# Giving each pair of heads its own order of TensorE work in a fused attention and rational-MLP kernel

## The chip, the cores and the metric

The kernel runs on one core of a Trainium2 chip. The metric is the device time of one execution in microseconds (us); the number compared is the median of several runs.

## The reference

Attention with a soft cap on the scores, over 4 batches of 12 heads, 448 positions and head dimension 64, feeds an MLP whose activation is a rational function.

```python
scores = scale * np.matmul(q, k.transpose(0, 1, 3, 2))
scores = cap * np.tanh(scores / cap)
scores = scores - np.max(scores, axis=-1, keepdims=True)
attn = np.exp(scores)
attn = attn / (np.sum(attn, axis=-1, keepdims=True) + 1e-09)
out = np.matmul(attn, v)                 # 4 x 12 x 448 x 64
x = out.transpose(0, 2, 1, 3).reshape(1792, 768)
h = x @ w_in                             # 768 x 2048
P = a[0] + a[1] * h + a[2] * h * h + a[3] * h * h * h
Q = 1.0 + abs(b[0]) * abs(h) + abs(b[1]) * h * h
y = (P / (Q + 1e-6)) @ w_out             # 2048 x 768
```

## The kernel before, in words

The kernel has two parts. **Attention** takes the 48 heads as 24 pairs, numbered from 0. For one pair, p, TensorE does these pieces, each of which is one entry in the kernel's lists:

- `k` and `q` (`prep_k`, `prep_q`): four transposes each (L343, L345, L366), which bring keys and queries of a pair to come into a score buffer. VectorE takes them out again in two instructions each (L350, L351, L381, L384), as a high and a low part.
- `s0`, `s1`, `s2` (`scores`, L429): the scores of 128 keys each, six matmuls of 448 columns that use half of the array's rows; they run two at a time, so six are three steps. Every odd pair has a fourth tile, `score3`, of twelve matmuls, for the last 64 keys of both pairs. ScalarE takes each tile out with a tanh (L440), and exponentiates it in place in SBUF (L457); VectorE adds a pair's tiles up for the softmax sums (L463).
- `pv` (L511): the product of a pair's exponentials with its values; `tails` (L528): the same for the fourth tile of two pairs. VectorE copies the results out (L535).
- `sums`, `sums4` (`norm`, `norm4`; L556, L594): the softmax sums of two or four pairs, which go through SBUF and a DRAM tensor `dn` and come back, inverted and broadcast, by DMA; VectorE multiplies with them (L627).

There are three score buffers in PSUM, printed as ps_127, ps_128 and ps_129 in the orders below (`slot`: an even pair's s0, s1, s2 go to the first, second and third; an odd pair's s0 to s2 and score3 to the second, third, first and second). The transposes for a later pair of the same parity use the first buffer when that pair is even, the third when it is odd. Two more banks, `pv` and `mi`, hold the products and the sums. Exponentials lie in a ring of six tiles, so two pairs of three. The early weights of the MLP are made ready between the pairs (L789 to L822).

The second part, the **MLP**, works in 32 units: `stage1` multiplies one 128-wide slice of `w_in` with 896 tokens (36 matmuls, 18 of 512 and 18 of 384 columns, each number split in a high and a low part so that three products are summed); `rational` computes the activation on ScalarE and VectorE; `stage2` multiplies with `w_out` (L928), and ScalarE or VectorE takes the result out (L955, L961). The first four units have nothing between their matmuls and are issued slice by slice (L858), the others in two halves (L843).

A planner, `Plan`, sets the order on each engine. Every operation is added with an engine, a cost in ns and the keys that it reads and writes; `flush` then walks a model of the engines in time, with a fixed latency between each two of them, and takes of the ready operations the one that was added first (some with a head start, `early`). All of TensorE's attention pieces write a common key, "turn", so that on TensorE they stand exactly in the order in which they were added; that order comes from `visits`, one fixed list for even pairs and one for odd ones:

```python
            if not p % 2:
                return [s0, s1, s2, *new, (pv, p - 1), (tails, p - 1)]
            sums = (norm, p // 2 - 1)
            ...
            four = [(norm4, p // 2 - 2)] * (p % 4 == 1)
            return [s0, s1, s2, (self.scores, p, 3), *four, (self.softmax, p, 3), *new, (pv, p - 1)]
```

`new` is the `k` and `q` of pair p + 2. In the first two pairs `fill` adds eight matmuls that compute nothing that is used (L405).

Of the kernel before, what the change touches and what calls it, by code (L numbers as in the profile page):

```python
# [23 lines left out]
NE = 6  # L24
# [22 lines left out]
WARM2 = (2, 1, 3)  # L47
FILL = (4, 4)
Q_ACT = ()
# [23 lines left out]
class Plan:  # L73
# [7 lines left out]
    def __init__(self):  # L81
        self.ops = []
        self.wr, self.rd = {}, {}
        self.n = 0
        self.free = [4500.0, 4600.0, 3700.0, 3700.0, 9900.0]
        self.dma_free = 11000.0
        self.where, self.over = {}, {}
# [160 lines left out]
class Body:  # L248
# [11 lines left out]
    def __init__(self, tc, io, cst, bounded):  # L260
# [15 lines left out]
        self.NG = self.NF // self.NCH  # L276
        self.plan = Plan()
        self.loaded = {(0, 0), ("v32", 0), ("v", 0)}
# [53 lines left out]
    def prep_k(self, p):  # L332
# [15 lines left out]
        self.busy(p, 0)  # L348
        self.op(PE, 440 + SHAPE_NS, tk, self.raw_keys(p, "rk"), [bk, "turn"], early=E_TR)
        self.op(DVE, dve_ns(512), lambda: nc.vector.tensor_copy(S[:, 1, :], pk), [bk], [K("kh")], early=E_PR)  # L350
# [3 lines left out]
    def prep_q(self, p):  # L354
# [18 lines left out]
        self.busy(p, 1)  # L373
        self.op(PE, 390, tq, self.raw_keys(p, "rq"), [bq, "turn"], early=E_TR)
        self.busy(p, 2)
# [25 lines left out]
    def fill(self, n):  # L401

        z = self.io["arena_r"][:, 0:512]
        for _ in range(n):
            self.op(PE, 213, lambda: self.nc.tensor.matmul(self.PS[0][:, 1], z[:, 0:128], z, start=True, stop=True),  # L405
                    [], [("ps", 0), ("psb", 0), "turn"])
# [8 lines left out]
    def scores(self, p, n):  # L415
# [8 lines left out]
        def run():  # L424
# [5 lines left out]
            return m  # L430
        first = n == 0 or p % 2 and n == 2
        self.op(PE, SC_NS * len(sets) + TURN_NS * first, run, [k for name, _ in sets for k in K(name)], w, early=E_SC)
# [18 lines left out]
    def exp(self, p, n, src, sk, e, ek):  # L451
# [7 lines left out]
        if n in (0, 3):  # L459
            return  # L460
        es, ks = self.es[p % NES], [("es", p % NES)]
        a, ak = self.etile(p, 0) if n == 1 else (es, None)
# [34 lines left out]
    def pv(self, p):  # L497
# [16 lines left out]

        self.op(PE, PV_NS + SHAPE_NS, run, [("rv", ring_of(g), 0)] + [t[1] for t in tiles], [pk, "turn"])

    def pv_tails(self, p):
# [13 lines left out]

        self.op(PE, TAIL_NS, run, [("v32", ring_of(g), 0), ("v32", ring_of(g), 1), ek], ["pv", "mi", "turn"])
        for x in range(2):
# [4 lines left out]
    def norm(self, k):  # L538
# [19 lines left out]

        self.op(PE, D_NS + SHAPE_NS, sums, [("es", (2 * k + x) % NES) for x in range(2)] + [tk, "ones"], [dk, "turn"])
        self.op(DVE, dve_ns(448), lambda: nc.vector.tensor_copy(DB, D), [dk], ["db"], early=E_EV)  # L560
# [19 lines left out]
    def norm4(self, k):  # L580
# [15 lines left out]

        self.op(PE, D4_NS + SHAPE_NS, sums, [*es, *(t[1] for t in tails), "ones"], [dk, "turn"])
        self.op(DVE, dve_ns(448), lambda: nc.vector.tensor_copy(DB, D), [dk], ["db"], early=E_EV)
# [42 lines left out]
    def attention(self):  # L641
# [33 lines left out]
        def visits(p):  # L675
# [10 lines left out]
            if p == 0:  # L686
                return [s0, s1, (k, 1), (q, 1), s2, (self.fill, FILL[0])]
            if p == 1:
                return [s0, (self.fill, FILL[1]), s1, (k, 2), s2, t, (q, 2), (k, 3), (q, 3), (pv, 0)]
            if not p % 2:  # L690
                return [s0, s1, s2, *new, (pv, p - 1), (tails, p - 1)]
            sums = (norm, p // 2 - 1)
            if p == P1 - 1:
                return [s0, s1, (pv, p - 1), sums, s2, t]
            four = [(norm4, p // 2 - 2)] * (p % 4 == 1)
            return [s0, s1, s2, (self.scores, p, 3), *four, (self.softmax, p, 3), *new, (pv, p - 1)]

# [127 lines left out]
    def stage1(self, u, between=None):  # L825
# [508 lines left out]
```

## Time and profile before

| what | us |
|---|---|
| runs of the kernel before | 659.46, 660.10, 660.89 |
| median | 660.1 |
| the profiled execution: its time | 659.91 |
| the profiled execution: its span, first to last instruction | 657.9 |
| TensorE (PE) busy in the span | 647.8 |
| VectorE (DVE) busy | 541.9 |
| ScalarE (ACT) busy | 442.2 |

The attention part ends on TensorE at 185.86 us of the span, the first four units at 214.47 us, the last matmul after 651 us. An engine's busy time counts a matmul until its modelled end, which overlaps the next one, so the length of a block of matmuls is best read as the time from its first start to the first start of the next block.

### The profile page before, as it was taken

Reading aid. Unit: us, or ns where it says so; the run is one execution under the profiler, and the core shown is the slowest. Engines: PE = TensorE matmul, PEld = TensorE weight load, DVE = VectorE, ACT = ScalarE, POOL = GpSimd, SP = SyncE. Lnnn points to the kernel's source line nnn. Section 1 sums busy time; section 2 is a strip of 40 time slices with the busy share of each in tenths; the row PEclk is TensorE's granted clock in tenths of the full one; section 3 lists DMA queues with packets and bytes.
Section 4 is the critical chain, followed back from the end, with each engine's and each line's share of the span. In section 5 each row is a group of like instructions: output and inputs, shape, how many; then the busy total and the mean of one; then the engine's idle time right before and its main releaser. Section 6 shows DMA issues by size and latency. Waiting matters only on the chain.

```text
span 657.9 us, 9767 instructions
## 1 busy us (share of the span) xinstructions
PE 647.8 (98%) x3820; PEld 542.0 (82%) x3820; DVE 541.9 (82%) x662; ACT 442.2 (67%) x531; POOL 85.0 (13%) x141
## 2 busy tenths in 40 slices
PE   8999999999999999999999999999999999999996
PEld 5555555655478899999999999999999999999996
DVE  4789899899679987977987897899699789969653
ACT  5899999999857867875457466646646565663560
POOL 4013222321200000020012002101200210120030
PEclk9999999999999999999999999999999999999999
DMA  7757864943230332195158118614821671481086
GB/s 170 186 138 171 203 163 100 199 119 85 59 86 22 128 141 92 51 197 113 48 106 158 49 49 152 158 43 86 166 68 49 128 142 60 95 170 33 1 139 203
DMA packets 79095, 74.45 MB, mean 113 GB/s; under 512 B 48456, under 2 KB 67264, under 8 KB 79040
## 3 DMA queue, kind: packets, MB, share of 16 engines
q1 hardware_dynamic: 68240, 48.68, 25.7%
q0 software_dynamic: 9648, 24.80, 22.5%
q8 instruction: 32, 0.52, 0.3%
q10 hardware_dynamic: 1152, 0.25, 0.2%
q14 instruction: 23, 0.19, 0.1%
HBM read 47.98 MB, written 25.65 MB: 112 GB/s over the span
## 4 chain that ended last, share of the span: by engine, by line
PE 82%; DVE 6%; ACT 4%; DMA 3%; issue 3%; POOL 0%; SPq 0%; DVEq 0%; POOLq 0%; ACTq 0%
PE ps L843 31%; PE ps L928 17%; PE mi L928 9%; PE pv L928 9%; PE ps L429 6%; PE mi L511 3%; DMA arena_r<-dn 2%; ACT etiles L440 2%; PE mi L594 1%; PE pv L511 1%; ACT etiles L457 1%; PE pv L528 1%; PE ps L343 1%; DMA dn<-arena_f 1%; PE ps L366 1%
## 5 line engine op out<-in xcount | busy, mean ns | idle before, releaser
L843 PE MATMUL ps<-arena_r,ring 128*128 128x512 f32 (+1 forms) x924 | 207.6, 363 | 0.0
L843 PEld LDWEIGHTS ps<-arena_r,ring 128*128 128x128 f32 x924 | 167.7, 188 | 17.5
L295 POOL DMA_DIRECT2D out_dram<-arena_f x49 | 42.0, 863 | 423.6 <-ACT arena_f L955 423.6
L928 PE MATMUL ps<-arena_r,etiles 128*128 128x384 f32 x462 | 89.7, 335 | 0.6 <-ACT arena_f L955 0.5
L457 ACT ACTIVATE etiles<-etiles,acap 128x896 f32<-128x896 f32 x84 | 85.5, 1053 | 0.2
L440 ACT ACTIVATE etiles<-ps 128x896 f32<-128x896 f32 x84 | 74.7, 921 | 13.9 <-PE ps L429 13.7
L928 PEld LDWEIGHTS ps<-arena_r,etiles 128*128 128x128 f32 x462 | 80.8, 188 | 1.3 <-ACT arena_f L955 0.8
L928 PE MATMUL mi<-arena_r,etiles 128*128 128x384 f32 x231 | 77.2, 336 | 0.0
L928 PE MATMUL pv<-arena_r,etiles 128*128 128x384 f32 x231 | 77.0, 335 | 0.0
L429 PEld LDWEIGHTS ps<-arena_r 64*128 64x128 f32 x576 | 51.0, 184 | 25.2 <-ACT etiles L457 7.8
L889 ACT ACTIVATE arena_f<-ps,b 128x896 f32<-128x896 f32 x32 | 32.3, 1009 | 54.8 <-PE ps L843 54.7
L429 PE MATMUL ps<-arena_r 64*128 64x448 f32 x576 | 67.7, 376 | 1.2 <-DVE arena_r L384 0.9
L789 ACT ACTIVATE arena_f<-arena_f 128x768 f32<-128x768 f32 x32 | 29.4, 918 | 44.1 <-DMA arena_f<-in_moe_w_out_dram 31.0
L901 ACT CAST etiles<-arena_f 128x896 fp32r<-128x896 f32 x32 | 30.3, 946 | 42.0 <-DVE arena_f L900 42.0
L893 DVE SCALAR_TENSOR_TENSOR arena_f<-arena_f,bab 128x896 f32<-128x896 f32 x32 | 36.8, 1150 | 23.8 <-ACT arena_f L890 23.8
L898 DVE SCALAR_TENSOR_TENSOR arena_f<-arena_f,one 128x896 f32<-128x896 f32 x32 | 36.7, 1148 | 11.3 <-ACT arena_f L896 11.3
L928 PEld LDWEIGHTS pv<-arena_r,etiles 128*128 128x128 f32 x231 | 43.3, 188 | 0.6
L928 PEld LDWEIGHTS mi<-arena_r,etiles 128*128 128x128 f32 x231 | 43.3, 188 | 0.6
L928 PE MATMUL ps<-ring,etiles 128*128 128x384 f32 x210 | 42.0, 334 | 0.0
L902 DVE TENSOR_TENSOR etiles<-arena_f,etiles 128x896 fp32r<-128x896 f32 x32 | 34.9, 1089 | 7.0 <-ACT etiles L901 6.8
L891 ACT ACTIVATE arena_f<-ps,a 128x896 f32<-128x896 f32 x32 | 35.3, 1104 | 3.5 <-DVE arena_f L899 3.5
L897 DVE SCALAR_TENSOR_TENSOR arena_f<-arena_f,a,ps 128x896 f32<-128x896 f32 x32 | 36.6, 1144 | 0.4
(145 smaller groups left out, 1124.2 us busy)
## 6 DMA issues: line engine op xcount, KB each, us to landing
out_dram<-arena_f POOLq DMA_DIRECT2D x49, 384.0 KB, 6.2
arena_f<-in_moe_w_out_dram SPq DMA_DIRECT2D x16, 768.0 KB, 4.3
arena_f<-in_moe_w_in_dram SPq DMA_DIRECT2D x16, 768.0 KB, 4.8
out_dram<-arena_f SPq DMA_DIRECT2D x13, 384.0 KB, 2.5
ring<-in_q_dram SPq DMA_DIRECT2D x44, 112.0 KB, 3.6
arena_r<-dn POOLq DMA_DIRECT2D x20, 224.0 KB, 5.3
ring<-in_k_dram SPq DMA_DIRECT2D x33, 128.0 KB, 3.1
ring<-in_v_dram SPq DMA_DIRECT2D x11, 384.0 KB, 3.7
```

Source lines behind the costliest of these rows:

```text
L295: self.op(eng, (625 if local else 450) if eng == SP else 1050, lambda: e.dma_start(out, in_, **accum), r, w, nbytes=nbytes, **kw)
L429: m = nc.tensor.matmul(self.PS[i][:, j, 0:448], st[r], mv[r], start=y == 0, stop=y == len(ops) - 1)
L440: self.op(ACT, act_ns(896, True), lambda: nc.scalar.activation(e, ps, AF.Tanh), pk + ["table"], [ek], early=E_TANH)
L457: self.op(ACT, act_ns(size, sk[0][0] == "ps", 1), lambda: nc.scalar.activation(e, src, AF.Exp, scale=acap), sk + ["table"], [ek])
L843: r = nc.tensor.matmul(po[:, ts], w[:, y, kc], mv, start=kc == 0 and z == 0, stop=kc == KC - 1 and z == 2)
L889: self.op(ACT, act_ns(n, True, 1), lambda: T.activation(Bt, h, AF.Abs, scale=b[:, 0:1]), hk, bk)
L891: self.op(ACT, act_ns(n, True, 2), lambda: T.activation(A, h, AF.Identity, scale=a[:, 3:4], bias=a[:, 2:3]), hk, ak)
L893: self.op(DVE, dve_ns(n, 1), lambda: stt(Bt, C, bab[:, 1:2], Bt, ALU.mult, ALU.add), ck + ["bab"], bk)
L897: self.op(DVE, dve_ns(n, 1), lambda: stt(A, A, a[:, 1:2], h, ALU.add, ALU.mult), hk, ak)
L898: self.op(DVE, dve_ns(n, 1), lambda: stt(Bt, Bt, one, C, ALU.add, ALU.mult), ck, bk)
L902: self.op(DVE, dve_ns(n), lambda: V.tensor_tensor(GL(), A, f32(GH()), ALU.subtract), ak + K("gh", ig), K("gl", ig))
L928: r = nc.tensor.matmul(po[n][:, 0:384], st, mv[:, 384 * n:384 * n + 384], start=(y == 0 and x == 0), stop=(y == self.NCH - 1 and x == 2))
```

## The change

The fixed lists give way to a table with one line for each pair, `ORDER`. A word is a piece, a number behind it says for which pair, relative to p: `k:2` are the keys' transposes for pair p + 2, `pv:-1` the product of pair p - 1. Three of its 27 lines stand here; the orders below show what the others come to. The exponentials of s0 and s1 become one instruction over 1792 columns. The costs that the planner reckons with are new, and one for a change of the kind of piece (`turn`) replaces fixed supplements. The first four units issue three matmuls in a row on 512 columns, then three on 384, where they alternated. Seven fill matmuls stand together in place of two times four.

```diff
-FILL = (4, 4)
+ORDER = {
+    0: "s0 s1 k:1 q:1 s2 fill:5",
+    1: "fill:2 s0 k:1 s1 s2 t k:2",
...
+    8: "s0 pv:-1 q:2 s1 s2 tails:-1",
...
+}
...
-SC_NS = 615
-TURN_NS = 200
-SHAPE_NS = 130
-PV_NS = 2220
-TAIL_NS = 870
-D_NS = 1430
-D4_NS = 2210
+SC_NS = 621
+SHAPE_NS = 165
+PV_NS = 2240
+TAIL_NS = 746
+D_NS = 1493
+D4_NS = 2240
...
+    def turn(self, shape):
+
+        old, self.last_shape = self.last_shape, shape
+        return SHAPE_NS * (shape != old)
...
-        if self.bounded:
+        if self.bounded and n == 1:
+            i = 3 * p % NE
+            both, keys = self.etiles[:, 896 * i:896 * i + 1792], [("e", i), ("e", i + 1)]
+            self.op(ACT, act_ns(1792, False, 1), lambda: nc.scalar.activation(both, both, AF.Exp, scale=self.c["acap"]),
+                    ["table"], keys)
+            self.add(p, n, e, ek)
+        elif self.bounded and n:
             self.exp(p, n, e, [ek], e, ek)
...
+            text = ORDER.get(p if p in ORDER else p - P1) or ORDER["odd" if p % 2 else "even"]
+            out = []
+            for w in text.split():
+                name, _, d = w.partition(":")
...
             def run(kc=kc, h=h, lo=lo):
                 w = wi().rearrange("p s (k f) -> p s k f", f=128)
-                for z, (y, mv) in enumerate(((0, h), (0, lo), (1, h))):
-                    for ts, x in zip(parts, mv):
-                        r = nc.tensor.matmul(po[:, ts], w[:, y, kc], x,
+                for ts, *x in zip(parts, h, lo, h):
+                    for z, y in enumerate((0, 0, 1)):
+                        r = nc.tensor.matmul(po[:, ts], w[:, y, kc], x[z],
```

**TensorE, pair 8.** Before: its three score tiles, the transposes for pair 10 into the first score buffer, then the product of pair 7 and its tails.

```order
L429 MATMUL ps_127<-arena_r 128x448 x6
L429 MATMUL ps_128<-arena_r 128x448 x6
L429 MATMUL ps_129<-arena_r 128x448 x6
L343 MATMUL ps_127<-ident,ring_142 128x128 x3
L345 MATMUL ps_127<-ident,ring_142 128x128
L366 MATMUL ps_127<-ident,ring_142 128x112 x4
L511 MATMUL mi<-etiles,ring_142 64x448 x6
L528 MATMUL pv<-etiles,ring_142 64x448
```

The same pair with the change (L461 scores, L553 product, L397 and L374 transposes, L570 tails):

```order
L461 MATMUL ps_127<-arena_r 128x448 x6
L553 MATMUL mi<-etiles,ring_142 64x448 x6
L397 MATMUL ps_127<-ident,ring_142 128x112 x4
L461 MATMUL ps_128<-arena_r 128x448 x6
L461 MATMUL ps_129<-arena_r 128x448 x6
L570 MATMUL pv<-etiles,ring_142 64x448
```

The product now stands between s0 and the transposes that reuse s0's buffer, the keys' transposes have gone to pair 9, and the three score tiles, one block before, are two.

**TensorE, from the transposes of pair 6 to the scores of pair 7.** Before, the product of pair 5 stood between them and the tails, and the fourth tile, of twelve matmuls, came last:

```order
L343 MATMUL ps_127<-ident,ring_141 128x128 x3
L345 MATMUL ps_127<-ident,ring_141 128x128
L366 MATMUL ps_127<-ident,ring_141 128x112 x4
L511 MATMUL mi<-etiles,ring_141 64x448 x6
L528 MATMUL pv<-etiles,ring_141 64x448
L528 MATMUL mi<-etiles,ring_141 64x448
L528 MATMUL pv<-etiles,ring_141 64x448
L528 MATMUL mi<-etiles,ring_141 64x448
L429 MATMUL ps_128<-arena_r 128x448 x6
L429 MATMUL ps_129<-arena_r 128x448 x6
L429 MATMUL ps_127<-arena_r 128x448 x6
L429 MATMUL ps_128<-arena_r 128x448 x12
```

With the change:

```order
L374 MATMUL ps_127<-ident,ring_141 128x128 x3
L376 MATMUL ps_127<-ident,ring_141 128x128
L397 MATMUL ps_127<-ident,ring_141 128x112 x4
L570 MATMUL pv<-etiles,ring_141 64x448
L570 MATMUL mi<-etiles,ring_141 64x448
L570 MATMUL pv<-etiles,ring_141 64x448
L570 MATMUL mi<-etiles,ring_141 64x448
L461 MATMUL ps_128<-arena_r 128x448 x6
L461 MATMUL ps_129<-arena_r 128x448 x6
L461 MATMUL ps_128<-arena_r 128x448 x12
L461 MATMUL ps_127<-arena_r 128x448 x6
```

The tails follow the transposes at once, and the fourth tile comes before s2, one tile behind the s0 that uses the same buffer.

**SyncE's queue at the end of attention.** The two last softmax sums (of pairs 20 and 21, then 22 and 23) go through this queue: four copies into SBUF rows, one write to `dn`, two broadcasts back. Before, a load of a `w_in` slice stood inside the first of the two:

```order
L295 DMA arena_f<-arena_f 8x1x56 x4
L295 DMA arena_f<-in_moe_w_in_dram 128x6x256
L295 DMA dn<-arena_f 32x56
L295 DMA arena_r<-dn 64x896 x2
L295 DMA arena_f<-arena_f 8x1x56 x4
```

With the change:

```order
L326 DMA arena_f<-arena_f 8x1x56 x4
L326 DMA dn<-arena_f 32x56
L326 DMA arena_r<-dn 64x896 x2
L326 DMA arena_f<-arena_f 8x1x56 x4
L326 DMA arena_f<-in_moe_w_in_dram 128x6x256
L326 DMA dn<-arena_f 32x56
L326 DMA arena_r<-dn 64x896 x2
```

The load now stands inside the second.

## Rows read from the trace of the kernel before

**Rows 1.** The page, part 1: busy time, share of the span and instructions of each engine.

```profile
PE 647.8 (98%) x3820; PEld 542.0 (82%) x3820; DVE 541.9 (82%) x662; ACT 442.2 (67%) x531; POOL 85.0 (13%) x141
```

**Rows 2.** Timeline of TensorE, a single score tile of pair 1: start, length, line, tiles, shape, count.

```profile
14.42 0.86 PE L429 MATMUL ps<-arena_r 64*128 64x448 f32 x6
15.21 0.55 PE L343 MATMUL mi<-ident,ring 128*128 128x128 f32 x3
```

**Rows 3.** Timeline of TensorE, an undisturbed pair (10) and the next one's scores.

```profile
80.48 2.10 PE L429 MATMUL ps<-arena_r 64*128 64x448 f32 x18
82.51 0.55 PE L343 MATMUL ps<-ident,ring 128*128 128x128 f32 x3
...
83.48 2.48 PE L511 MATMUL mi<-etiles,ring 128*64 128x448 f32 x12
...
86.80 3.38 PE L429 MATMUL ps<-arena_r 64*128 64x448 f32 x30
```

**Rows 4.** Timeline of TensorE, disturbed pairs 2, 8 and 12; idle time and its releaser in brackets.

```profile
21.58 1.49 PE L429 MATMUL ps<-arena_r 64*128 64x448 f32 x12
23.47 0.88 PE L429 MATMUL ps<-arena_r 64*128 64x448 f32 x6 [0.40 <-DVE arena_r L384]
24.28 0.55 PE L343 MATMUL ps<-ident,ring 128*128 128x128 f32 x3
...
63.80 2.09 PE L429 MATMUL ps<-arena_r 64*128 64x448 f32 x18
66.67 0.55 PE L343 MATMUL ps<-ident,ring 128*128 128x128 f32 x3 [0.78 <-ACT etiles L440]
...
93.49 2.09 PE L429 MATMUL ps<-arena_r 64*128 64x448 f32 x18
95.66 0.55 PE L343 MATMUL ps<-ident,ring 128*128 128x128 f32 x3
```

**Rows 5.** Waits of TensorE over the span: who, for whom, us in total, times, longest.

```profile
PE ps L429 <- DVE arena_r L384: 0.9, 3, 0.4
```

**Rows 6.** Timeline of ScalarE, the first two tanhs of pair 11.

```profile
87.72 1.73 ACT L440 ACTIVATE etiles<-ps 128x896 f32<-128x896 f32 x2 [1.00 <-PE ps L429]
```

**Rows 7.** Timeline of VectorE: the last of the four instructions that empty pair 12's transposes.

```profile
85.64 0.67 DVE L384 SCALAR_TENSOR_TENSOR arena_r<-ps,c,arena_r 128x448 fp32r<-128x448 f32 x1
```

**Rows 8.** Timeline of TensorE: the first four units, and a later unit's halves.

```profile
185.86 14.31 PE L858 MATMUL ps<-arena_r,ring 128*128 128x512 f32 x68
...
214.47 1.21 PE L928 MATMUL ps<-arena_r,etiles 128*128 128x384 f32 x6
...
304.03 3.28 PE L843 MATMUL ps<-arena_r,ring 128*128 128x384 f32 x18
307.15 0.33 PE L928 MATMUL pv<-ring,etiles 128*128 128x384 f32 x1
...
311.31 2.47 PE L843 MATMUL ps<-arena_r,ring 128*128 128x512 f32 x10
313.62 0.39 PE L843 MATMUL ps<-extra,ring 128*128 128x512 f32 x1
```

**Rows 9.** Timeline of VectorE, SyncE's queue and TensorE where the MLP begins.

```profile
192.19 1.16 DVE L627 TENSOR_TENSOR arena_f<-arena_r,arena_f 128x448 f32<-128x448 f32 x2 [3.50 <-DMA arena_r<-dn]
...
183.28 0.35 SPq L295 DMA_DIRECT2D dn<-arena_f  x1
186.03 1.16 SPq L295 DMA_DIRECT2D arena_r<-dn  x2
194.06 0.33 SPq L295 DMA_DIRECT2D dn<-arena_f  x1
195.42 1.15 SPq L295 DMA_DIRECT2D arena_r<-dn  x2
...
216.56 1.58 PE L928 MATMUL ps<-arena_r,etiles 128*128 128x384 f32 x6
...
219.73 2.38 PE L928 MATMUL ps<-arena_r,etiles 128*128 128x384 f32 x12 [0.53 <-ACT arena_f L955]
```

More of the change, by code (lines that the diff above doesn't have):

```diff
@@ L84, in __init__ @@
         self.n = 0
-        self.free = [4500.0, 4600.0, 3700.0, 3700.0, 9900.0]
-        self.dma_free = 11000.0
+        self.free = [4500.0, 4600.0, 3700.0, 3700.0, 8800.0]
+        self.dma_free = 10000.0
         self.where, self.over = {}, {}
@@ L277, in __init__ @@
         self.plan = Plan()
+        self.last_shape = None
         self.loaded = {(0, 0), ("v32", 0), ("v", 0)}
@@ L348, in prep_k @@
         self.busy(p, 0)
-        self.op(PE, 440 + SHAPE_NS, tk, self.raw_keys(p, "rk"), [bk, "turn"], early=E_TR)
+        self.op(PE, 427 + self.turn("k"), tk, self.raw_keys(p, "rk"), [bk, "turn"], early=E_TR)
         self.op(DVE, dve_ns(512), lambda: nc.vector.tensor_copy(S[:, 1, :], pk), [bk], [K("kh")], early=E_PR)
@@ L373, in prep_q @@
         self.busy(p, 1)
-        self.op(PE, 390, tq, self.raw_keys(p, "rq"), [bq, "turn"], early=E_TR)
+        self.op(PE, 380 + self.turn("k"), tq, self.raw_keys(p, "rq"), [bq, "turn"], early=E_TR)
         self.busy(p, 2)
@@ L403, in fill @@
         z = self.io["arena_r"][:, 0:512]
+        self.last_shape = "k"
         for _ in range(n):
-            self.op(PE, 213, lambda: self.nc.tensor.matmul(self.PS[0][:, 1], z[:, 0:128], z, start=True, stop=True),
+            self.op(PE, 235, lambda: self.nc.tensor.matmul(self.PS[0][:, 1], z[:, 0:128], z, start=True, stop=True),
                     [], [("ps", 0), ("psb", 0), "turn"])
@@ L430, in run @@
             return m
-        first = n == 0 or p % 2 and n == 2
-        self.op(PE, SC_NS * len(sets) + TURN_NS * first, run, [k for name, _ in sets for k in K(name)], w, early=E_SC)
+        self.op(PE, SC_NS * len(sets) + self.turn("s"), run, [k for name, _ in sets for k in K(name)], w, early=E_SC)
     def softmax(self, p, n):
@@ L460, in exp, with add @@
             return
+        self.add(p, n, e, ek)
+    def add(self, p, n, e, ek):
+        nc = self.nc
         es, ks = self.es[p % NES], [("es", p % NES)]
@@ L513, in run @@
             return m
-        self.op(PE, PV_NS + SHAPE_NS, run, [("rv", ring_of(g), 0)] + [t[1] for t in tiles], [pk, "turn"])
+        self.op(PE, PV_NS + self.turn("pv"), run, [("rv", ring_of(g), 0)] + [t[1] for t in tiles], [pk, "turn"])
     def pv_tails(self, p):
@@ L530, in run @@
             return m
-        self.op(PE, TAIL_NS, run, [("v32", ring_of(g), 0), ("v32", ring_of(g), 1), ek], ["pv", "mi", "turn"])
+        self.op(PE, TAIL_NS + self.turn("tails"), run, [("v32", ring_of(g), 0), ("v32", ring_of(g), 1), ek], ["pv", "mi", "turn"])
         for x in range(2):
@@ L557, in sums @@
             return m
-        self.op(PE, D_NS + SHAPE_NS, sums, [("es", (2 * k + x) % NES) for x in range(2)] + [tk, "ones"], [dk, "turn"])
+        self.op(PE, D_NS + self.turn("sums"), sums, [("es", (2 * k + x) % NES) for x in range(2)] + [tk, "ones"], [dk, "turn"])
         self.op(DVE, dve_ns(448), lambda: nc.vector.tensor_copy(DB, D), [dk], ["db"], early=E_EV)
@@ L595, in sums @@
             return m
-        self.op(PE, D4_NS + SHAPE_NS, sums, [*es, *(t[1] for t in tails), "ones"], [dk, "turn"])
+        self.op(PE, D4_NS + self.turn("sums"), sums, [*es, *(t[1] for t in tails), "ones"], [dk, "turn"])
         self.op(DVE, dve_ns(448), lambda: nc.vector.tensor_copy(DB, D), [dk], ["db"], early=E_EV)
@@ L685, in visits @@
                         (tails, p), (norm, p // 2)]
[L686 to L696, printed above, removed]
+            text = ORDER.get(p if p in ORDER else p - P1) or ORDER["odd" if p % 2 else "even"]
+            out = []
+            for w in text.split():
+                name, _, d = w.partition(":")
+                d = int(d or 0)
+                if name in ("k", "q") and p + d >= P1 or name == "sums4" and p % 4 != 1:
+                    continue
+                out.append(dict(s0=s0, s1=s1, s2=s2, t=t, k=(k, p + d), q=(q, p + d), pv=(pv, p + d), tails=(tails, p + d),
+                                sums=(norm, p // 2 - 1), score3=(self.scores, p, 3), tanh3=(self.softmax, p, 3),
+                                sums4=(norm4, p // 2 - 2), fill=(self.fill, d))[name])
+            return out
         for p in range(P1):
```

22 rows, old and new, of the table ORDER are left out of this document.

## The prediction

> **What bounds the kernel now.** I first read the page's table of busy times: TensorE has work for 647.8 of 657.9 us [rows 1]. What another engine saves is therefore worth nothing unless TensorE waits for it, and the change takes no matmul away but one fill. But "busy" hides waits here, since a matmul's modelled end covers the start of the next. So I next read TensorE's timeline block by block, from first start to first start of the next block. In attention the blocks repeat to the hundredth. A block of three score tiles that nothing disturbs takes 82.51 - 80.48 = 2.03 us, the eight transposes after it 83.48 - 82.51 = 0.97 [rows 3], a score tile by itself 15.21 - 14.42 = 0.79 [rows 2]. Three tiles in a row are thus cheaper than three alone: (2.03 - 0.79) / 2 = 0.62 for each further tile, and 0.79 - 0.62 = **0.17 us for the entry into a block of scores and the way out of it**.
>
> Against these lengths the disturbed blocks stand out. Pair 2's lasts 24.28 - 21.58 = 2.70 us, 0.67 too long: its third tile waits for VectorE to empty the transposes that lie in its buffer. Pair 8's lasts 2.87, 0.84 too long: the transposes wait for the tanh of s0. Pair 12's lasts 2.17, 0.14 too long, without an idle time that the view shows [rows 4]; three more of the eleven even pairs have this 0.13 to 0.14. The list of waits has three of the first sort, 0.9 us idle in all [rows 5]; at 0.67 of length for 0.40 of idle that is about 1.5 us. Together **the waits lengthen attention by about 1.5 + 0.84 + 4 x 0.14 = 2.9 us**. After attention TensorE goes on without a gap until `stage2` begins; there it is idle for 0.53 us, and six matmuls shortly before take 1.58 where the first six took 1.21, 0.37 more [rows 8, 9]: 0.9 us in all.
>
> **The change, part by part.** The sum is made against the profiled execution, 659.91 us; the median of the runs is 0.2 above it.
>
> More blocks: the orders, counted from the first lone score tile to the units, have 95 blocks before and 107 after: scores +11, transposes and fill +3, products -1, and the six unit matmuls that stood between two attention blocks have joined the others, -1. At 0.17 each that is 12 x 0.17 = **+2.0 us**. No row shows a product directly behind transposes or a tail behind scores; bounds are 0.1 and 0.2 each, the rows' spread for the change between other kinds, so +1.2 to +2.4. One fill matmul of 512 columns less: -0.23, at the unit's step for that width [rows 8].
>
> Waits that go: with `pv` between s0 and the transposes that need its buffer, or between a pair's transposes and the tile that needs theirs, each of the waits above is covered by a block of over 2 us. The order does this in pairs 2, 4, 6, 8, 10, 14, 16, 18 and 20; in pair 12 the old order stays. **-2.9 + 0.1 = -2.8 us**; bounds -2.9, and 0 if every wait comes back elsewhere.
>
> Waits that come: a buffer may be written again when the tanh that reads it has ended. Pair 11's first tanh starts 87.72 - 86.80 = 0.92 us after its block of scores [rows 3, 6]; two tanhs take 1.73, so the first ends some 0.9 after its start, and its buffer is free 1.8 to 1.9 us after the block's. The fourth tile, third in line behind s0, would come 0.10 + 3 x 0.61 = 1.93 us after it: just covered. In pairs 7 and 11 the new order puts it directly behind s1, 1.3 us after the start, and in pair 19 s1 follows the previous pair's s2, which uses its buffer, at the same distance. That is three times 1.9 - 1.3 = 0.6, less what a slow start of the block itself takes: **+1.6 us**. Bounds: 0, if the tiles before them run late anyhow; 3 x 1.4 if ScalarE is one tanh behind.
>
> The merged exponential shortens ScalarE's work, which ends no wait on TensorE but pair 8's, counted above. It also delays the first exponential until both tanhs are done; whoever needs it, VectorE's sum and `pv`, comes a tile later in all orders: 0. It holds ScalarE in one piece, so a tanh that comes meanwhile starts up to 0.9 later; where a buffer is needed soon, the order keeps all three tanhs ahead of it: 0.
>
> VectorE's emptying of the transposes: the last of its four instructions ends 85.64 + 0.67 - 83.48 = 2.83 us after the transposes [rows 3, 7]. Before, 3.8 or 4.7 us of other blocks stood between; now in eight places 2.9 to 3.8. I walked VectorE's order through pairs 4 to 18 with the durations of its instructions: its queue is never more than one instruction behind where this counts. So 0, with 8 x 0.33 = 2.6 at the other end (worked out under the rivals).
>
> Units: the 138 matmuls from 185.86 to 214.47 take 207 ns each, alternating between 512 and 384 columns. A later unit shows both widths in runs: 3.12 us for 18 of 384, 173 ns, and 2.31 for ten of 512, 231 ns [rows 8]. Three of each are 1.212 us against 6 x 0.207 = 1.244, and there are 24 such groups: **-0.75 us**; bounds 0 and -0.9. The Trainium skill (TensorE: Matmul & The Clock Gate, Part 3, What overlaps and what doesn't) says that a weight load overlaps matmuls under way only when it goes to other rows of the array. All these loads go to all 128 rows; by that rule load and matmul would stand one behind the other and their order would not matter, so the sum would be 0.75 us higher. The trace has them overlap at 173 ns a step, so I go by the rows.
>
> The start of the MLP: VectorE waits 3.50 us, until 192.19, for the broadcast of the sums of pairs 20 and 21, and what it does next, the last inputs and the first units' activations, is late for `stage2`. Of that chain the write to `dn` took 186.03 - 183.28 = 2.75 us with the load of a weight slice before it, against 195.42 - 194.06 = 1.36 in the next one, without [rows 9]. The load leaves this chain and joins the later one. I take three quarters of the 0.9 us that TensorE loses there: **-0.7 us**; bounds -0.9 and 0, if the later sums are now delayed as much.
>
> Sum: 2.0 - 0.23 - 2.8 + 1.6 - 0.75 - 0.7 = -0.9. The fourth tile of the other odd pairs, which just fails to be covered now, gains some 0.3 in four or more of them: about -1.2 in all, so 658.7 us against the profiled execution and 658.9 against the median. **Forecast 658.8 us.**
>
> **The rivals.**
>
> *All waits go (657.0).* The three new places cost nothing, since the buffer's release comes with the tile before it, and the MLP's delay goes whole, 0.2 more: 660.1 - 1.2 - 1.6 - 0.2 = 657.1, or 657.0 with the few hundredths of the fourth tiles. For it: ScalarE has idle time before almost every block of scores, 1.00 us at pair 11 [rows 6]. Against it: that idle time is itself the wait for TensorE, so the tanh cannot be earlier.
>
> *VectorE's queue decides (661.4, slower).* The transposes of pairs 6, 10, 14, 16 and 18 now stand one short block of tails ahead of the scores that follow. If VectorE, busy 541.9 of 657.9 us [rows 1], is 1 us behind when they come, their buffer is free after 3.8 us, against 2.9 to 3.8 of cover, 3.5 on average: 8 x 0.33 = 2.6, so 661.4. It decides from 0.1 us behind in the tightest place and 0.7 on average; pair 2's wait was of this sort [rows 4]. The Trainium skill (TensorEngine Tiling, Key Properties) says that changing the tiling mode drains TensorE, which speaks against every further block; the trace agrees with 0.17 us each, already in the sum.
>
> *The MLP takes the gain (659.5).* The weight load now delays the last softmax sums, and `stage2` starts no earlier: 658.8 + 0.7.
>
> *The order does nothing (660.1).* The waits that go and the blocks and waits that come are equal, and the units' matmuls are as fast alternating: 659.9 to 660.1.
>
> **How the numbers follow.** A measurement of this kernel can tell about 0.2%, 1.3 us, from no change, so the forecast lies on that bound. Forecast 0.42, half of it on either side; all waits go 0.24, faster; MLP takes the gain 0.12 and the order does nothing 0.08, both no change; VectorE decides 0.14, nearly all slower. Faster 0.45, same 0.42, slower 0.13. The range reaches from the first rival to the low half of VectorE's: 657.0 to 660.9.
>
> **What would show it.** Right: pair 8's block of scores without an idle row; a fourth tile of pairs 7 and 11 that starts 0.5 or 0.6 late; lone score tiles at 0.79; the first four units in 29.1 us for 144 matmuls; attention ending near 185. Wrong: waits of TensorE on L384's successor in many pairs; units still at 207 ns; an idle time of TensorE at the start of `stage2` above 0.53 us.

## The result, and the profile after

The change made the kernel slower: 664.16 us median of 6 runs (663.76 to 666.16) against 660.08 of 6 (659.00 to 660.89), a ratio of 1.0062 with a 95% interval of 1.0047 to 1.0078. The prediction, 658.8 in a range of 657.0 to 660.9, was wrong in sign and size. The profiled execution took 664.07 us with a span of 662.2 us, by the unrounded spans 4.2 us more than the profiled execution before.

Part 1 of the page and TensorE's waits over the span, with the change:

```profile
PE 649.7 (98%) x3819; PEld 541.8 (82%) x3819; DVE 541.9 (82%) x662; ACT 440.4 (67%) x507; POOL 85.2 (13%) x141
...
PE ps L461 <- ACT etiles L471: 2.5, 4, 1.2
PE w L1334 <- DVE arena_r L1306: 1.5, 1, 1.5
PE ps L397 <- DVE arena_r L381: 0.5, 1, 0.5
PE ps L461 <- DVE arena_r L382: 0.3, 1, 0.3
```

The waits of [rows 5] have gone, and four of score tiles on a tanh (L471) have come, of which there were none. I read TensorE block by block again, from first start to first start; blocks that nothing disturbs are as long as before, to 0.01 or 0.02 us. Attention ends at 187.87, where the first units begin; before, the six unit matmuls inside it taken off (1.41 us), at 184.45. Where the 4.2 us come from, by these two executions:

| | predicted | measured |
|---|---|---|
| twelve more blocks, one fill less | +1.8 | +1.65 |
| waits that go (pairs 2, 4, 8, 9, 12, 16, 17, 18, 20) | -2.8 | -3.0 |
| waits that come at pairs 7, 11 and 19 | +1.6 | +1.8 |
| a wait at pair 17 | 0 | +1.5 |
| a wait at the end of pair 1 | 0 | +0.7 |
| fourth tiles; small waits in pairs 5, 10 and 15 | -0.3 | +0.45 |
| a later start of the first scores | 0 | +0.17 |
| units in runs of three | -0.75 | -0.36 |
| start of the MLP | -0.7 | -1.05 |
| one weight load that lands late | 0 | +0.53 |
| SyncE's end, after the last matmul | 0 | +1.86 |
| sum | -1.2 | +4.2 |

Two rows of the table are differences between single executions and not the change's doing: the first scores start anywhere from 7.62 to 8.43 us in the fourteen profiles shown here, and the late weight load does not come in e1, which has the same order.

The three predicted waits (pairs 7, 11 and 19) look alike. TensorE in pair 7, where the fourth tile waits, and in pair 17, where s1 waits three times as long:

```profile
57.18 1.49 PE L461 MATMUL ps<-arena_r 64*128 64x448 f32 x12
59.08 2.09 PE L461 MATMUL ps<-arena_r 64*128 64x448 f32 x18 [0.40 <-ACT etiles L471]
61.09 0.55 PE L374 MATMUL ps<-ident,ring 128*128 128x128 f32 x3
...
129.80 0.87 PE L461 MATMUL ps<-arena_r 64*128 64x448 f32 x6
131.91 1.49 PE L461 MATMUL ps<-arena_r 64*128 64x448 f32 x12 [1.25 <-ACT etiles L471]
133.33 1.71 PE L636 MATMUL mi<-arena_f 128*32 128x448 f32 x16
```

Five tiles take 61.09 - 57.18 = 3.91 us in place of 3.31; pair 17's three take 3.53 in place of 2.02. ScalarE, then VectorE, then GpSimd there:

```profile
129.27 1.78 ACT L680 CAST arena_r<-arena_f 128x896 fp32r<-128x896 f32 x2 [1.51 <-DVE arena_f L669]
130.95 0.91 ACT L471 ACTIVATE etiles<-ps 128x896 f32<-128x896 f32 x1
...
125.50 0.68 DVE L415 SCALAR_TENSOR_TENSOR arena_r<-ps,c,arena_r 128x448 fp32r<-128x448 f32 x1
128.61 1.16 DVE L669 TENSOR_TENSOR arena_f<-arena_r,arena_f 128x448 f32<-128x448 f32 x2 [2.43 <-DMA arena_r<-dn]
129.69 0.68 DVE L412 TENSOR_SCALAR arena_r<-ps,c 128x448 fp32r<-128x448 f32 x1
...
117.00 0.54 POOL L326 DMA_DIRECT2D dn<-arena_f  x1
122.11 2.07 POOL L326 DMA_DIRECT2D arena_r<-dn  x4 [3.98 <-DMA dn<-arena_f]
```

VectorE stands for 2.43 us before its multiplications (L669) with a broadcast of the softmax sums; behind them is the emptying of pair 18's transposes (L412 on). ScalarE's queue has two casts (L680) of what L669 produces, and the tanh that frees s1's buffer, that of pair 16's s2, stands behind them. The broadcast was issued from 122.11, after GpSimd had waited 3.98 us for the write to `dn`. Which of the two queues holds TensorE, these rows cannot say.

The second part begins without the idle time and the long six matmuls of [rows 9], and the broadcast leaves 1.39 us after the write to `dn`:

```profile
186.34 0.34 SPq L326 DMA_DIRECT2D dn<-arena_f  x1
187.73 1.16 SPq L326 DMA_DIRECT2D arena_r<-dn  x2
...
217.36 1.21 PE L970 MATMUL ps<-arena_r,etiles 128*128 128x384 f32 x6
219.45 1.20 PE L970 MATMUL ps<-arena_r,etiles 128*128 128x384 f32 x6
221.57 2.37 PE L970 MATMUL ps<-arena_r,etiles 128*128 128x384 f32 x12
```

The end of the program, shown by the instructions of its last line (duration minimum, median and maximum in ns, then first and last start), before and with the change, and the page's row for SyncE's instruction fetches (packets, MB):

```profile
L1322 SPq EVENT_SEMAPHORE  x14: 17/28/28, 656.3 to 657.9; - x14
q14 instruction: 23, 0.19, 0.1%
```

```profile
L1364 SPq EVENT_SEMAPHORE  x14: 17/28/28, 658.5 to 662.1; - x14
q14 instruction: 24, 0.20, 0.1%
```

SyncE closes the program with a chain of fourteen short instructions. It took 1.6 us, and now 3.6: by the starts of its records, the fifth comes 2.08 us after the fourth (658.69 to 660.77), where 0.06 is usual. One more packet of code was fetched on SyncE's queue. With the change SyncE runs 320 instructions, 12 fewer than before (332), so the chain lies 12 instructions earlier in its code.

### The profile page after: what moved, and what is told of

The parts are those of the page before. It is cut to its first block, busy times and chain, and to the rows that moved or that the text cites. A ratio compares the mean times of both kernels' runs of the same rounds, so it can differ in the third digit from the quotient of the medians.

```text
span 662.2 us, 9722 instructions
## 1 busy us (share of the span) xinstructions
PE 649.7 (98%) x3819; PEld 541.8 (82%) x3819; DVE 541.9 (82%) x662; ACT 440.4 (67%) x507; POOL 85.2 (13%) x141
## 4 chain that ended last, share of the span: by engine, by line
PE 91%; DMA 3%; ACT 2%; issue 2%; DVE 1%; POOL 0%; POOLq 0%; ACTq 0%; DVEq 0%; SPq 0%
PE ps L885 30%; PE ps L970 17%; PE mi L970 9%; PE pv L970 9%; PE ps L461 8%; PE ps L900 4%; PE pv L553 4%; PE mi L553 4%; DMA arena_f<-in_moe_w_out_dram 1%; PE mi L636 1%; PE pv L570 1%; PE ps L397 1%; PE ps L374 1%; ACT etiles L471 1%; DMA arena_r<-dn 1%
## 5 line engine op out<-in xcount | busy, mean ns | idle before, releaser
L471 ACT ACTIVATE etiles<-ps 128x896 f32<-128x896 f32 x84 | 73.4, 916 | 16.8 <-PE ps L461 15.8
L461 PE MATMUL ps<-arena_r 64*128 64x448 f32 x576 | 70.9, 379 | 2.8 <-ACT etiles L471 2.5
L461 PEld LDWEIGHTS ps<-arena_r 64*128 64x128 f32 x576 | 50.6, 185 | 26.5 <-ACT etiles L471 7.3
L475 ACT ACTIVATE etiles<-etiles,acap 128x1792 f32<-128x1792 f32 x24 | 43.1, 1796 | 0.4
L494 ACT ACTIVATE etiles<-etiles,acap 128x896 f32<-128x896 f32 x36 | 36.9, 1047 | 0.4
```

The costliest lines, as they stand in the source:

```text
L461: m = nc.tensor.matmul(self.PS[i][:, j, 0:448], st[r], mv[r], start=y == 0, stop=y == len(ops) - 1)
L475: self.op(ACT, act_ns(1792, False, 1), lambda: nc.scalar.activation(both, both, AF.Exp, scale=self.c["acap"]), ["table"], keys)
L494: self.op(ACT, act_ns(size, sk[0][0] == "ps", 1), lambda: nc.scalar.activation(e, src, AF.Exp, scale=acap), sk + ["table"], [ek])
```

## The experiments

"Attention ends" is the start of the first unit matmul after it. All runs but e4, e8, e10 and e11 have the changed kernel's order.

**e1, the end.** Drains are added to the branch that is not taken, so only the place of the closing chain in SyncE's code moves:

```diff
             Body(tc, io, c, False).run()
+            for _ in range(12):
+                nc.sync.drain()
```

> The changed kernel with 12 drain instructions of SyncE added at the end of the branch that is not taken, so that nothing more is executed and SyncE's closing chain lies 12 instructions further on, as in the kernel before. Theory (the closing chain is split by a border between two fetched pieces of code): the gap of 2.05 us inside the chain goes, there are 23 instruction packets on SyncE's queue in place of 24, and the time falls by 1.9 to 2.1, to about 662.1 us. Rival (the last stores are late, the chain waits for them): the chain still has a gap of about 2 us and the time stays near 664.1.

```profile
L1366 SPq EVENT_SEMAPHORE  x14: 17/28/28, 657.9 to 659.9; - x14
q14 instruction: 23, 0.19, 0.1%
```

661.74 us, ratio 1.0030 [1.0019, 1.0042] to the kernel before: about half of the loss is gone. The gap is gone too (0.06 us there; another of 0.5 us, further on, waits for the last store), and so is the packet. In all runs below but e11 the chain lies there too (in e4 two instructions further on), with drains where they are needed, so the runs with the change's order are compared with e1.

**e11, the same in the kernel before,** with 244 drains:

> The kernel before with 244 drains at the end of SyncE's branch that is not taken, which puts its closing chain where the changed kernel had it, 12 instructions short of its old place, if fetched pieces of code are 128 or 256 instructions long. Nothing more is executed. Theory (a chain that lies across such a border waits for a fetch): the chain gets a gap of 1.5 to 2.2 us after its fourth instruction and the time rises by that, to about 661.5 to 662. Rival (the gap of the changed kernel came from its stores or its own shorter queue): no gap, and the time stays within 0.5 us of the kernel before.

```profile
L1324 SPq EVENT_SEMAPHORE  x14: 17/28/28, 656.5 to 660.1; - x14
q14 instruction: 24, 0.20, 0.1%
```

662.03 us, ratio 1.0033 [1.0019, 1.0046], from code that never runs. The gap, 2.02 us, lies after the fourth instruction again. So the place of the chain is shown as the cause. That it lies across the border of two fetched pieces of code is not shown by itself; the extra packet and the distance (244 and 12 make 256 instructions) fit it.

**e2, pair 17: ScalarE's casts behind the tanh.**

```diff
-... scalar.activation(e, ps, AF.Tanh), pk + ["table"], [ek], early=E_TANH)
+... scalar.activation(e, ps, AF.Tanh), pk + ["table"], [ek, ("tanh", p, n)], early=E_TANH)
...
-... scalar.copy(XH, x), keys, hk)
+... scalar.copy(XH, x), keys + [("tanh", 16, 2)] * (kc > 1), hk)
```

> As the run with the shifted end, and in ScalarE's queue the two casts of MLP inputs that stood ahead of the tanh of pair 16's third tile stand behind it; TensorE's order is the same. Theory (that tanh, and so pair 17's second tile, waits for the casts, which wait for VectorE and a broadcast): TensorE's wait of 1.25 us at pair 17 goes, its blocks of scores there take 2.02 and not 3.54, attention ends 1.3 to 1.5 us earlier, near 186.4, and the time is 1.3 to 1.5 below the shifted end's, near 660.7. Rival (VectorE itself is the late one there): the wait moves to the next tile or to the scores that need the transposes of pair 19, and attention ends within 0.4 us of 187.9.

TensorE and ScalarE there, and what TensorE waits for now:

```profile
128.85 0.92 ACT L471 ACTIVATE etiles<-ps 128x896 f32<-128x896 f32 x1 [1.24 <-PE ps L461]
...
129.65 1.49 PE L461 MATMUL ps<-arena_r 64*128 64x448 f32 x12
132.03 0.88 PE L461 MATMUL ps<-arena_r 64*128 64x448 f32 x6 [0.89 <-DVE arena_r L382]
```

The tanh now runs at 128.85, and nothing is gained: s2 waits for VectorE instead, the block takes 3.44 us, attention ends at 187.62, the time is 661.81 us (1.0032). The theory fell and the rival held; ScalarE's queue alone was not the cause.

**e5, VectorE's multiplications behind the emptying as well.** The last line of the edit moves one multiplication from pair 15 to pair 16.

```diff
-... [("bc", i, x, j) for j in range(2)], [("u0", p), ("u1", p)])
+... [("bc", i, x, j) for j in range(2)] + [(self.qset(18)[0], "ql")] * (p in (8, 9)), [("u0", p), ("u1", p)])
...
-for _ in range((1 + (p == P1 - 1 and self.bounded)) * (m == 3) if todo else 0):
+for _ in range((1 + (p == P1 - 1 and self.bounded) + (p == 16) - (p == 15)) * (m == 3) if todo else 0):
```

> As the run with the casts held, and VectorE's two multiplications of pairs 8 and 9 with the broadcast sums, which stood ahead of the emptying of pair 18's transposes, stand behind it. Theory (both queues, ScalarE's and VectorE's, held pair 17 up behind one broadcast that had not landed, and either was enough): now neither waits for it there, pair 17's block of three score tiles takes 2.0 to 2.2 us and not 3.4 or 3.5, attention ends 1.2 to 1.4 us earlier than with the casts held, near 186.3. Rival (the pair is late for another reason, such as the emptying itself, which takes 2.8 us after the transposes and has one block of tails and two score tiles of cover, 2.2): the block takes 2.6 us or more and attention ends later than 186.8.

```profile
129.58 2.09 PE L461 MATMUL ps<-arena_r 64*128 64x448 f32 x18
131.63 1.71 PE L636 MATMUL mi<-arena_f 128*32 128x448 f32 x16
```

The block takes 2.05 us: both queues stood behind the one broadcast. VectorE's was enough by itself (e2); that ScalarE's was too, one reads from s1's wait until 131.91 in the change's own rows, and it was not tried alone. Attention ends at 186.20. But the time rose to 664.58 (1.0068). VectorE, SyncE's queue and TensorE at the start of the second part:

```profile
193.88 0.24 DVE L611 TENSOR_SCALAR arena_f<-arena_f,guard 32x56 f32<-32x56 f32 x1 [2.90 <-DMA arena_f<-arena_f]
...
187.39 2.00 SPq L326 DMA_DIRECT2D arena_f<-arena_f  x3
189.43 1.47 SPq L326 DMA_DIRECT2D arena_r<-dn  x2
190.94 0.67 SPq L326 DMA_DIRECT2D arena_f<-arena_f  x1
...
219.41 0.98 PE L970 MATMUL ps<-arena_r,etiles 128*128 128x384 f32 x4 [1.47 <-ACT etiles L943]
221.37 0.62 PE L970 MATMUL ps<-arena_r,etiles 128*128 128x384 f32 x2 [0.98 <-DVE etiles L944]
224.42 2.38 PE L970 MATMUL ps<-arena_r,etiles 128*128 128x384 f32 x12 [1.39 <-ACT arena_f L997]
```

With other times the planner has put three of the four copies of the last sums ahead of the broadcast of the sums before, which leaves at 189.43, 1.7 us later than with the change though attention ended 1.7 earlier; and on VectorE the inversion of the last sums (L611), which waits for the fourth copy, ahead of the multiplications with that broadcast. The activations come late, and TensorE, which had no such waits with the change, has 1.47 + 0.98 + 1.39 us of them.

**e9, that end put back in order** (two dependences for the planner and one for the weight load; the two multiplications ahead of the last sums):

```diff
+            for t in [t for t in todo if t is not None]:
+                self.xout(t)
+            todo.clear()
             norm(P1 // 2 - 1)
...
-... ["db"],
+... ["db"] + [("dn", 1 - k % 2)] * end,
...
-        self.op(DVE, 740, small, ["guard"], keys)
+        self.op(DVE, 740, small, ["guard"] + [(u, 2 * k - x) for u in ("u0", "u1") for x in (1, 2)] * end, keys)
...
-                self.load_w(todo[u + 1][1], todo[u + 1][0])
+                self.load_w(todo[u + 1][1], todo[u + 1][0], [("bc", (self.B * self.NP // 2 - 2) % len(self.BC), 0, 0)] * (u == 0))
```

> As the run with the queue of pair 17 mended, and the end of attention put back in the order that the changed kernel had there: on SyncE the copies of the last sums behind the broadcast of the sums before them, on VectorE the inversion of the last sums behind the multiplications with that broadcast, and the weight load behind that broadcast too. Theory (the 1.4 us gained in attention was lost again because the planner, with other times, interleaved these two chains): attention ends at 186.2, the waits of TensorE on the first activations go, the first twelve-matmul group of the second half starts at 219 to 219.6 in place of 221.8, and the time is 660 to 661, 1 to 1.5 below the shifted end's. Rival (VectorE's work between attention and the second half is the bound whatever its order): that group starts at 220.5 or later and the time stays above 661.7.

(What this text and that of e10 call the group of twelve is the nineteenth matmul of the second half: 217.98 before, 220.49 with the change, 221.82 in e5.)

```profile
217.82 1.53 PE L974 MATMUL ps<-arena_r,etiles 128*128 128x384 f32 x6
220.93 2.35 PE L974 MATMUL ps<-arena_r,etiles 128*128 128x384 f32 x12 [0.54 <-ACT arena_f L1001]
```

The nineteenth starts at 219.19, in the range, with attention ending at 186.24, 1.62 us before e1's. Of this the time shows little: 661.44 us (1.0027 [1.0017, 1.0037]). From the nineteenth to the last matmul this profiled execution took 1.8 us longer than e1's, 435.1 against 433.3. Of that 0.7 us come at once, and belong to the start of the MLP: the twelve matmuls at 220.93 wait 0.54 us for an eviction (L1001), so they start only 0.6 us before e1's (221.55). The other 1.1 us are one wait near 526 us, behind a weight load that landed late. So the order of the two chains was part of what e5 lost; another part stayed. Over all runs here this stretch lies between 433.3 and 435.6 us.

**e3, the fourth tile behind s2 (pairs 7, 11), s2 ahead of the tails (pair 18).**

```diff
-    7: "sums4 s0 s1 score3 s2 k:2 ...",   11: "s0 s1 score3 s2 sums4 ...",   18: "... q:2 tails:-1 s2",
+    7: "sums4 s0 s1 s2 score3 k:2 ...",   11: "s0 s1 s2 score3 sums4 ...",   18: "... q:2 s2 tails:-1",
```

> As the run with the shifted end, and in pairs 7 and 11 s2 comes before the fourth tile, in pair 18 s2 before the tails. Theory (a buffer is free 1.8 to 1.9 us after its block starts, and the new order came back to it after 1.3): the block of five tiles of pairs 7 and 11 takes 3.3 in place of 3.9 us, that of pairs 18 and 19 loses its 0.6 for one more block at 0.17, attention ends 1.6 us earlier, near 186.3, the time 1.6 below the shifted end's, near 660.5. Rival (ScalarE's five tanhs pace these tiles in any order): the blocks stay within 0.2 us of 3.9, and the time within 0.5 of 662.1.

```profile
57.21 1.50 PE L461 MATMUL ps<-arena_r 64*128 64x448 f32 x12
59.00 2.10 PE L461 MATMUL ps<-arena_r 64*128 64x448 f32 x18 [0.29 <-DVE arena_r L415]
61.03 0.55 PE L374 MATMUL ps<-ident,ring 128*128 128x128 f32 x3
```

The blocks stay at 3.82 and 3.74 us, as the rival had it, but not for its reason: ScalarE no longer holds the block, VectorE does. s2's buffer holds transposes with only a block of tails and two score tiles behind them; with the transposes that late, s2 waits in the third place as the fourth tile did. Pairs 18 and 19 win 0.08 us: the extra block costs its 0.17, and of the 0.60 that the scores of pair 19 were too long 0.34 stay. Attention ends at 187.46, and the time is 661.47 us (1.0021).

**e7, pair 1's transposes in the old order,** and **e12,** the same edit on e9, where pair 17 does not wait:

```diff
-    1: "fill:2 s0 k:1 s1 s2 t k:2",       2: "q:0 q:1 pv:-2 s0 s1 pv:-1 s2 q:2",
+    1: "fill:2 s0 k:1 s1 s2 t q:1 k:2",   2: "q:1 pv:-2 s0 s1 pv:-1 s2 q:2",
```

> The changed kernel with the shifted end and, at the end of pair 1, the queries of pair 2 transposed before the keys of pair 3, as in the old order. Theory (the queries of pair 3 wait for VectorE's first read of the keys of pair 3, which lie in the same buffer, because a block stands between the two): the twelve transposes take 1.36 and not 2.04 us, and attention ends 0.6 to 0.7 us earlier, at 187.2. Rival (VectorE is late there with anything): the wait comes back at pair 2's tiles, and attention ends within 0.2 of 187.9.

> The kernel of the run with the end in order, in which pair 17 no longer waits, with the edit of the run on pair 1. Theory (while pair 17 waited for a broadcast, whatever was gained ahead of it only lengthened that wait): now the 0.68 us of pair 1 arrive at the end of attention, which comes 0.6 to 0.7 us earlier than 186.24, at 185.5 to 185.7, counted from the same start of the first scores. Rival (some other place takes it up, such as the next sums): attention ends within 0.2 us of 186.2.

e7, pair 1 and pair 17:

```profile
17.70 0.60 PE L397 MATMUL mi<-ident,ring 112*128 112x112 f32 x4
...
19.05 1.35 PE L553 MATMUL pv<-etiles,arena_f 128*64 128x448 f32 x6
...
129.47 0.87 PE L461 MATMUL ps<-arena_r 64*128 64x448 f32 x6
131.82 1.49 PE L461 MATMUL ps<-arena_r 64*128 64x448 f32 x12 [1.48 <-ACT etiles L471]
```

The twelve transposes take 1.35 us, as in the old order. In e7 attention still ends at 187.80, as the first scores started 0.25 later than in e1 and pair 17 waits 1.48 in place of 1.2. In e12 it ends at 185.47, 0.77 before e9 from a start 0.10 earlier. So the 0.68 us are real and arrive only where pair 17 does not wait for a broadcast. The times are of one run each, 662.61 and 660.13 us, and settle nothing.

**e4, the old order with the merged exponential and the units in threes,** and **e6, the change with two exponentials:**

```diff
-        if self.bounded and n == 1:
-            ...
-        elif self.bounded and n:
+        if self.bounded:
             self.exp(p, n, e, [ek], e, ek)
```

> The kernel before with two parts of the change, the merged exponential and the units in runs of three, and with the old order and the old planner's costs. Theory (the loss is the order's alone, and these two parts are small gains): attention ends within 0.3 us of the kernel before's, the first four units' matmuls take 205 ns each and not 207, the idle 0.53 us at the start of the second half stays, and the time is 0.3 to 0.6 us below the kernel before, near 659.6. Rival A (the merged exponential holds ScalarE and delays tanhs): TensorE has new waits on ScalarE in attention and it ends 1 us or more later. Rival B (a weight load does not overlap a matmul, so their order is worth nothing): 207 ns a matmul and no gain.

> The changed kernel with the shifted end and two exponentials again where one stood; TensorE's order is that of the change. Theory (the merged exponential saves ScalarE 0.2 us a pair and so takes 0.83 off attention under the old order; it helps the new one as well): attention ends 0.3 to 1 us later than with the shifted end, at 188.2 to 188.9, with more waits of TensorE on tanhs. Rival (holding ScalarE in one piece of 1.8 us is what makes tanhs late in pairs 7, 11 and 19): their blocks of 3.9, 3.9 and 4.5 us become 3.3 to 3.6 and attention ends earlier than 187.5.

Attention ends at 185.03 in e4, 0.83 earlier than in the kernel before, six unit matmuls in both, where 0.3 was expected at most; the extra 0.13 us of four even pairs (4, 12, 16 and 20; [rows 4] have that of 12) is gone, 2.02 in each. In e6 it ends at 189.14, 1.28 later than in e1 and so later than expected, with new waits in pairs 9 and 15. The nineteenth matmul of its second half starts 2.2 us later than e1's (222.66 against 220.48), and the time is 664.43 us (1.0067). In attention the merged exponential is worth about a microsecond in either order. e4's time, 660.34 (1.0010 [0.9998, 1.0023]), shows no gain: its twelve runs spread from 658.65 to 662.96, and part is lost where the second part begins.

**e8 and e10, the old order with repairs.** What e8 puts into its table (the lines that it takes out are left out here):

```diff
+    1: "fill:2 s0 k:1 s1 s2 t q:1 k:2 q:2 pv:-1",
+    2: "s0 s1 pv:-1 s2 q:2",
+    3: "k:1 s0 tails:-2 s1 score3 tanh3 s2 k:2 q:2 pv:-1",
+    'even': "s0 s1 s2 k:2 q:2 pv:-1 tails:-1",
+    'odd': "s0 s1 s2 score3 sums4 tanh3 k:2 q:2 pv:-1",
+    8: "s0 s1 s2 pv:-1 k:2 q:2 tails:-1",
+    9: "s0 s1 sums4 s2 score3 tanh3 k:2 q:2 pv:-1",
```

e10 is without lines 8 and 9, with e9's end.

> The changed kernel's code with the old order in its table, but for six places: the fill in one block, the product of pair 1 between s1 and s2 of pair 2, transposes for pair 4 on either side of pair 3's first tile, the product ahead of the transposes in pair 8, the sums ahead of s2 in pair 9, and the end of the last pair as in the change. Theory (blocks at 0.17 us each and the few waits of the old order are all there is): attention ends at 180.5 to 181.5 us, against 184.5 before (without the six unit matmuls) and 187.9 with the change, and the time is 655.5 to 657.5. Rival (the end of attention only hands the time on: the last softmax sums and VectorE's queue set the start of the second half): attention ends as early, but the gaps at the start of the second half grow by 1 us or more and the time is 657.5 to 659.

> As the run of the old order mended, with pairs 8 and 9 in the old order again (the product ahead of the transposes and the sums ahead of s2 had cost 2.7 us there) and with the end of attention as in the run with the end in order. Theory: attention ends near 182.3 us, against 184.5 before without the six unit matmuls, the first twelve-matmul group of the second half starts at 215 to 216 against 219.73 in the kernel before, and the time is 656 to 657.5, below both kernels. Rival (VectorE's chain from the last but one sums sets that start): it starts at 217.5 or later, and the time is 658 to 660.

In e8 the repair of pairs 8 and 9 cost 2.7 us. TensorE there, and the row of a view by stretches (it ends with the granted clock of TensorE as a share of full speed, the share of the DMA engines and GB/s):

```profile
72.84 0.57 PE L620 MATMUL mi<-extra,arena_f 128*32 128x448 f32 x2 [2.13 <-DVE arena_f L561]
...
76.34 2.61 PE L445 MATMUL ps<-arena_r 64*128 64x448 f32 x18
78.88 0.55 PE L358 MATMUL ps<-ident,ring 128*128 128x128 f32 x3
...
74.00:76.00 2.00, 2.00 (x16) 0.35 (x8) 1.55 (x2) 0.01 (x1) 0.00 (x0) 0.51 0.81 215
```

`sums4`, moved up, waits 2.13 us for VectorE's copies; VectorE itself had stood 2.06 us for a broadcast just before (L653, until 68.25), as in pair 17. After this wait TensorE's granted clock, 1.00 until 74 us, was 0.51 from 74 to 76, the lower of its two levels (1.2 and 2.4 GHz), and 1.00 again from 78. The sums took 76.34 - 72.84 = 3.50 us in place of 2.39 and the 18 score matmuls after them 2.54 in place of 2.02, so 1.63 of the 2.7 us are the clock's. Attention ended at 185.03, and the second part began as in e5. The time was 662.27 us, a median over two groups: four of the ten runs took 659.89 to 660.61 at a mean clock of 0.997 to 0.999, six 661.80 to 663.50 at 0.991 to 0.995. In the other profiles here the clock did not fall in attention. In e10:

```profile
218.17 2.38 PE L956 MATMUL ps<-arena_r,etiles 128*128 128x384 f32 x12 [0.55 <-ACT arena_f L983]
```

Attention ends at 182.74, 5.1 us before the change's. The nineteenth matmul starts at 216.41, 1.6 us before that of the kernel before and between the theory's range and the rival's, and the group of twelve at 218.17 against 219.73 [rows 9]. 658.83 us, ratio 0.9981 [0.9971, 0.9992]: faster than both kernels, by 0.2% than the kernel before, and in the rival's range, not in the 656 to 657.5 expected. What each of its parts gives was not tried apart.

## Why the prediction was wrong

**The step that failed** is that on VectorE's emptying: its queue "never more than one instruction behind where this counts". I had added up durations and left out that the multiplication with a broadcast (L669; L627 before) can stand at the head of the queue and wait for a DMA. The profile before shows such a wait of VectorE, just ahead of the emptying of pair 18's transposes:

```profile
126.72 0.62 DVE L627 TENSOR_TENSOR arena_f<-arena_r,arena_f 128x448 f32<-128x448 f32 x1 [2.25 <-DMA arena_r<-dn]
```

What the runs showed in place of the 0: a wait of 1.5 us of TensorE at pair 17, behind 2.43 us of VectorE, that goes when the emptying stands ahead of the multiplications (e5: the block takes 2.05 us). Pair 16 was one of the five places named, though not only tails but also its s2 stands between its transposes and the scores of pair 17. The rival "VectorE's queue decides" had a late VectorE, but not the wait for a DMA behind it, and put it at 0.33 in eight places, not at 1.5 in one. ScalarE's casts wait for the same broadcast (129.27 in the rows of pair 17).

**Waits that come** were found in one way only, a score tile that returns to a buffer. The three found measured 0.6 each. Pair 1's, transposes that wait for a read of the other half of their buffer, was missed (e7, e12), and so were three of 0.1 to 0.2. The rest of attention was right: blocks at 0.17, and the waits that go, -3.0 for -2.8, though in part in other pairs than named (9, 12 and 17; pairs 6, 10 and 14 had none to lose).

**The end of the program** was in no term. It comes from the place of SyncE's closing chain, 12 instructions earlier, and not from TensorE's order as such; at 1.9 us it is nearly half of the loss (e1, e11).

**Units:** the mechanism was right, the size off by half. 144 matmuls took 217.36 - 187.87 = 29.49 us, 204.8 ns each against 207.3; by the starts of the records the three steps on 512 columns take 236, 234 and 230 ns and the three on 384 take 172, 176 and 180, where the sum took 231 and 173 from the later unit. Their weight loads take 188 ns each and go to all 128 rows, so load and matmul do overlap here. That speaks against the rule of the Trainium skill (TensorE: Matmul & The Clock Gate, Part 3, What overlaps and what doesn't), from which the prediction worked out that the order is worth nothing.

**Merged exponential:** sized 0, worth 0.8 to 1.3 us of attention (e4, e6). I had looked only for waits that the views show, and the even pairs' 0.13 us, which show no idle time, went with it.

**Start of the MLP:** -1.05 for -0.7, and the rows fit the reason given, 1.39 us from the write to the broadcast; but only in that one interleaving. In e5 and e8 the rival "the MLP takes the gain" came true, by SyncE's and VectorE's order at the end of attention.

## What to carry to other kernels

Where a planner sets the order, a change of order or of its costs moves every queue: for each one, look for an instruction that waits for a DMA with something that TensorE needs behind it. A gain ahead of such a wait is worth nothing until the wait is gone (e7, e12), and a gain at the end of a stage is worth what the next stage's first inputs allow (e5, e9). A wait of TensorE can cost more than its own length: behind e8's 2.13 us the lower clock took another 1.63. Compare two kernels' ends before explaining a difference of 2 us: code that is shorter by a few instructions can cost as much.

## What the runs showed of the hardware

A chain of SyncE's shortest instructions, 0.06 us each, stopped for 2.0 us after the fourth in both kernels whose chain lay at that place, and in none of the other twelve profiles; one more code packet was fetched each time. The Trainium skill (Runtime: NRT & Kernel Launch, Instruction fetch mechanics) says that the step from one fetched block to the next is mostly hidden, and that a taken branch breaks the prefetch; this chain lies behind a branch, and if such a step is what stops it, it is not hidden here.

Single runs of one kernel differ by up to 4.3 us (e4), more than most edits here are worth. In e8 a spread of 3.6 us goes with the granted clock. Weight loads that land late can be another part. ScalarE and the weight loads of TensorE with the change, where one came late:

```profile
525.04 0.89 ACT L831 ACTIVATE arena_f<-arena_f 128x768 f32<-128x768 f32 x1 [7.64 <-DMA arena_f<-in_moe_w_out_dram]
...
526.36 0.19 PEld L970 LDWEIGHTS pv<-arena_r,etiles 128*128 128x128 f32 x1 [0.37 <-ACT arena_f L997]
```

Against TensorE's place this load landed 1.3 us later than in the kernel before; ScalarE's evictions behind it were late, and TensorE lost the 0.53 us of the table. In e1's profile it did not.
